# Where a chunked-attention and feed-forward kernel issues the adds of its second block's partial results

## The chip, the cores and the metric

The kernel runs on one core of a Trainium2 chip. The metric is the device time of one execution in microseconds (us); several executions are timed, and their median is given. Of one execution there is also a profile with a trace of every instruction and DMA.

## The reference

The attention works on chunks of 64 tokens (eight batches, eight heads, 576 tokens, head size 64); its output `x` has 4608 rows of 512, and goes through a feed-forward layer with a hidden size of 2048 and a PReLU:

```python
scores = scale * np.matmul(q_c, k_c.transpose(0, 1, 2, 4, 3))
scores = scores - np.max(scores, axis=-1, keepdims=True)
attn = np.exp(scores)
attn = attn / (np.sum(attn, axis=-1, keepdims=True) + 1e-09)
out = np.matmul(attn, v_c)
...
h = x @ w_in
g = np.maximum(h, 0.0) + alpha * np.minimum(h, 0.0)
return (g @ w_out).astype(np.float32)
```

## The kernel before

Tokens are worked on in nine blocks of 512. The first three ("plain" blocks 0, 1 and 2) compute the feed-forward layer directly; the other six are worked on in three pairs with a seven-product (Strassen-like) scheme, whose combined weights are made while the plain blocks run. All matrix products are done in three passes on values split into a high and a low part.

The plain part is a list of 48 steps `(phase, block, f)`: in one step `ffn_in` (L311) multiplies `x` with the f-th 128 columns of `w_in`, `prelu` (L300 to L303) and a split into `gh` and `gl` (L323, L324) follow on ScalarE and VectorE, and `ffn_out` (L336) of the step two places earlier adds into four PSUM banks `ps_o`. Blocks 0 and 1 take turns in four phases, since the weights arrive as they go: each is interrupted once, its four sums are put aside in DRAM (`partial`), and when the block's second part ends, the new sums are added to these by DMAs that GpSimd issues with `accum_op=add`. `store` (L345) copies the four banks into SBUF: the first two into the two halves of a buffer `more`, the third into `ob`, the fourth into `g`. The fourth is added at once (L374). The first three go into the list `adds` (L372) and are issued later, one at a time.

Beside these steps run, at fixed step numbers, "visits" (L396) of the attention of later blocks. A visit runs on TensorE the values product of the tile two visits back (L272, which reads the transposed probabilities `pT` and writes the two PSUM tiles `ps_a`) and the scores of a new tile (L194, into the same two tiles). Then come on VectorE the row maxima (L210) and their scaling (L211), on ScalarE eight exponentials (L214, each followed by a read of its sum), on VectorE the division (L216 to L218), on ScalarE a copy of the values' product out of PSUM (L288), on VectorE a transpose of 32 by 32 blocks (L225), and on SP's queue eight DMAs into `pT` (L232) and one load of `v`. The next visit writes both `ps_a` tiles anew, and so needs L214, L288 and L210 of the last to be done.

At the steps named in `COMBINE` (L806) `combine` (L512) makes two new weight tiles. It adds high and low parts of two tiles (L520), forms four combinations (L527 to L530), and for each of the two tiles casts it into a buffer (L536, ScalarE), puts the rest beside it (L537, VectorE) and stores its two halves to DRAM by two DMAs of GpSimd (L498 in `keep_a`). The buffer is one of two named `raw`, or `raw`, `raw`, `more` in rotation (L533) where `early` is false, so a cast waits until the stores of an earlier tile out of the same buffer have landed. Behind each tile's two stores one entry of `adds` is issued, if there is one:

```python
            for half, s in zip((left, right), name):
                stored = keep_a(side, {1: 5, 2: 6, 3: 7, 4: 3}[s], j, w[:, :, half])
            if adds:
                to, what = adds.pop(0)
                with tc.issue_after(stored.ins):
                    nc.gpsimd.dma_start(out=to, in_=what, accum_op=ALU.add)
```

The order on each engine is set by a list scheduler from priorities and its own model of durations; TensorE's part from step 20 on is pinned to the program's order. Each engine executes its list in order. GpSimd's DMAs run in one queue and share the chip's DMA engines with SP's and ScalarE's. The first block's three adds are issued in the combinations at steps 29 and 30, the second block's in those at steps 35 and 36; `wo_640`, `wo_705` and `wo_766` below belong to steps 36, 37 and 39.

Of the kernel before, what the change touches and what calls it, by code (L numbers as in the profile page):

```python
# [27 lines left out]
def tile_local_attention_prelu_ffn(  # L28
# [44 lines left out]
    def f32(t):  # L73
        return t.bitcast(F32)
# [66 lines left out]
    def prepare(f, behind=None):  # L141
        with tc.issue_after(behind.ins) if behind else nullcontext():
            wi[f] = split_weight("wi", f)
            wo[f] = split_weight("wo", f)
# [10 lines left out]
    def attn_load(s, parts="qkv", other=None):  # L155
        if "q" in parts:
            q_sb, kb = (load.tile([P, H, C], F32, name=name) for name in ("q_sb", "k_sb"))
            for t, src in ((q_sb, qT), (kb, kT)):
                (other or nc.sync).dma_start(out=t, in_=src[:, s].rearrange("p (h t) -> p h t", t=C))
            qkv[s] = [q_sb, kb, None]  # L160
        if "v" in parts:
            v_sb = load.tile([P, DM], F32, name="v_sb", bufs=2)
            loads.append(nc.sync.dma_start(out=v_sb, in_=v[:, s]))
            qkv[s][2] = v_sb
# [178 lines left out]
    adds = []  # L343

    def store(acc, b, keep):  # L345
        for t, o in enumerate(acc):
            rows = slice(b * TB + t * P, b * TB + (t + 1) * P)
            before = partial.get((b, t))
            if b == PLAIN - 1:
                ob = const.tile([P, DM], F32, name=f"wi{NF - 2 - t}")  # L350
            elif keep and b == 0:
                side = "wi" if t % 2 else "wo"
                ob = const.tile([P, DM], F32, name=f"{side}{NF - 1 - t // 2}")
            elif keep:
                pool, name = ((load, "q_sb"), (load, "v_sb"), (load, "v_sb"), (soft, "pr"))[t]
                ob = pool.tile([P, DM], F32, name=name, bufs=2 if name == "v_sb" else 1)
            elif t < 2:
                if t == 0:
                    both = stage.tile([P, 2, DM], F32, name="more", bufs=1)
                ob = both[:, t]  # L360
            elif t == 2:
                ob = stage.tile([P, DM], F32, name="ob", bufs=1)
            else:
                ob = gp.tile([P, DM], F32, name="g")
            with tc.high_priority(offset=HIGH):
                nc.scalar.copy(ob, o)  # L366
            if keep:
                partial[b, t] = dram.tile([P, DM], F32, name=f"partial{b}_{t}")
                nc.sync.dma_start(out=partial[b, t], in_=ob)
            elif before is not None:  # L370
                if t < 3:
                    adds.append((before, ob))  # L372
                else:
                    nc.gpsimd.dma_start(out=before, in_=ob, accum_op=ALU.add)  # L374
                finals.append((out[rows, :], before))
            else:
                nc.sync.dma_start(out=out[rows, :], in_=ob)

    def new_x():
        return (xp.tile([P, NK, TB], F32R, name="xh"), xp.tile([P, NK, TB], F32R, name="xl"))  # L380
# [6 lines left out]
    def attend(part, s):  # L387
        with tc.high_priority(offset=HIGH):
            if part == 0:
                attn_softmax(s, attn_scores(s))  # L390
            elif part == 1:
                attn_transpose(s) if s < EARLY else attn_blocks(s)
            else:
                attn_x(s, attn_values(s))
# [101 lines left out]
    def keep_a(side, i, j, a):  # L496
        n, u = unit(side, i, j)
        return nc.gpsimd.dma_start(out=units[side][n][:, u], in_=f32(a))  # L498
# [3 lines left out]
    def keep_quarters(f):  # L502

        j, second = f % JF, f >= JF
        keep_a("wi", 4 if second else 1, j, wi[f][:, :, halves[second]])
        keep_a("wo", 4 if second else 1, j, wo[f][:, :, halves[second]])
        if second:
            keep_a("wo", 2, j, wo[f][:, :, halves[0]])
        else:
            keep_a("wi", 2, j, wi[f][:, :, halves[1]])  # L510

    def combine(side, j, early):  # L512

        ws = wi if side == "wi" else wo
        pair = [ws[j], ws[JF + j]]
        left, right = halves
        a = []
        for w in pair:
            t = stage.tile([P, 512], F32, name="t1")
            nc.vector.tensor_tensor(t, f32(w[:, 0]), f32(w[:, 1]), op=ALU.add)  # L520
            a.append(t)
        a11, a22 = a[0][:, left], a[1][:, right]
        if side == "wi":
            a12, a21 = a[0][:, right], a[1][:, left]
        else:
            a21, a12 = a[0][:, right], a[1][:, left]
        nc.vector.tensor_tensor(a22, a21, a22, op=ALU.add)  # L527
        nc.vector.tensor_tensor(a21, a11, a21, op=ALU.subtract)
        nc.vector.tensor_tensor(a11, a22, a11, op=ALU.subtract)
        nc.vector.tensor_tensor(a12, a12, a11, op=ALU.subtract)  # L530
        names = ((2, 4), (3, 1)) if side == "wi" else ((2, 3), (4, 1))
        for t, name in zip(a, names):
            which = "raw" if early else ("raw", "raw", "more")[fetched[0] % 3]  # L533
            fetched[0] += 1
            w = stage.tile([P, 2, 512], F32R, name=which, bufs=2 if which == "raw" else 1)
            nc.scalar.copy(w[:, 0], t)  # L536
            nc.vector.tensor_tensor(w[:, 1], t, f32(w[:, 0]), op=ALU.subtract)  # L537
            for half, s in zip((left, right), name):
                stored = keep_a(side, {1: 5, 2: 6, 3: 7, 4: 3}[s], j, w[:, :, half])
            if adds:  # L540
                to, what = adds.pop(0)
                with tc.issue_after(stored.ins):
                    nc.gpsimd.dma_start(out=to, in_=what, accum_op=ALU.add)

# [247 lines left out]
    def new_raw(b):  # L792
        for n, name in enumerate(("xh", "xl")):
            x[b + n] = xp.tile([P, NK, TB], F32, name=name)

    COMBINE = (20, 22, 23, 24, 26, 29, 30, 31, 33, 35, 36, 37, 39, 40, 41, 43)
    combined = [(side, j) for side in ("wi", "wo") for j in range(JF)]
    ops, conversion = {}, []
    for n, (p, b, f) in enumerate(steps):
        _, f0, f1 = phases[p]  # L800
        if f == f0:
            acc = []
            if p >= 3 and b + 1 < PLAIN:
                x[b + 1] = new_x()
        if n == 2 * NF:
            new_raw(PLAIN)  # L806
        if n == n0 + 1:

            tick = nc.gpsimd.tensor_copy(out=table, in_=f32(x[1][1])[:, 0, TB - 1:])
        if n0 < n <= n0 + NF:  # L810
            with tc.issue_after(tick.ins):
                keep_quarters(n - n0 - 1)
        pinned[0] = n >= 20
        if n == len(steps) - 1:
            with tc.issue_after(loads[-1].ins):
                while finals:
                    dst, src = finals.pop(0)
                    nc.sync.dma_start(out=dst, in_=src)
        for st, s in beside[n]:
            attend(st, s)  # L820
        if 2 * n in late:
            if 2 * n == visits[0]:
                attn_load(late[2 * n][1], "q")
            visit(*late[2 * n])
        if ready < NF:
            prepare(ready, done_x.get({2: SPB, 3: SPB + 2, 4: SPB + 3}.get(ready)))
            ready += 1
        elif n in COMBINE:

            with tc.issue_after(stages["softmax"][0].ins), tc.issue_after(stages["softmax"][1].ins):  # L830
                combine(*combined.pop(0), 23 <= n <= 36)
        if n == len(steps) - 8:
            ops, conversion = convert(PLAIN)
        if len(steps) - 8 <= n < len(steps) - 4:
            conversion.pop(0)()
        pending.append((acc, ffn_in(x[b], f), f, f0, f1, b, False))
        if 2 * n + 1 in late:
            visit(*late[2 * n + 1])
        if n >= len(steps) - 3:

            with tc.issue_after(stages["split"][0].ins):
                for _ in range(3):
                    conversion.pop(0)()

        if len(pending) > (1 if n < 20 else 2):
            second(*pending.pop(0))
# [9 lines left out]
    for pair in range(NPAIR):  # L856
        b = PLAIN + 2 * pair
# [53 lines left out]
```

## Time and profile before

| | |
|---|---|
| median of three runs | 839.68 us |
| lowest and highest of them | 834.14 and 841.08 us |
| the profiled execution | 837.25 us |
| its span from first to last instruction | 835.5 us |
| TensorE matmul busy | 806.1 us (96%) |
| TensorE weight load busy | 644.8 us (77%) |
| VectorE busy | 671.0 us (80%) |
| ScalarE busy | 542.8 us (65%) |
| GpSimd busy | 215.7 us (26%) |
| moved by DMA | 192.40 MB, mean 230 GB/s |
| chain that ended last | TensorE 83%, ScalarE 4%, DMA 4%, VectorE 3%, SP's queue 3% |

The first line is what counts; the others are of one execution, whose times are read against its own 837.25 us. Matmuls overlap, so the shares say which engine is busy, not how near it is to its peak.

### The profile page before, as it was taken

The page shows a single profiled execution, that of the slowest core. Times are in us where ns is not written, and L with a number is a line of the kernel's source. Part 1 is how long each engine was busy: PE and PEld are TensorE (multiplying, and loading weights), DVE is VectorE, ACT ScalarE, POOL GpSimd, SP SyncE. Part 2 cuts the span into 40 slices and gives each one's busy share as a digit, 9 for nine tenths or more (in the row PEclk, how much of TensorE's full clock was granted, in tenths as well). Part 3 has the DMA queues.
Part 4 walks back from the last instruction along what each step waited for, and adds up shares of the span by engine and source line. Part 5 has one row for each costly group of instructions (what it writes and reads, how often), then busy time and mean ns, then how long its engine had stood idle before and what let it go on. Part 6 is the DMA issues. An engine that isn't in the chain of part 4 may idle for free.

```text
span 835.5 us, 15368 instructions
## 1 busy us (share of the span) xinstructions
PE 806.1 (96%) x5248; PEld 644.8 (77%) x5248; DVE 671.0 (80%) x1268; ACT 542.8 (65%) x1392; POOL 215.7 (26%) x340
## 2 busy tenths in 40 slices
PE   4799999999989899999999999999999999999998
PEld 3577888777768678787788788787887888888886
DVE  5899999979769888677688996777789966568875
ACT  5985666657666576677876555687765546566452
POOL 4006223224324432111112242111122422111232
PEclk9999999999999899999999999999999999999999
DMA  9629777656687868687876799786557995555788
GB/s 277 215 78 343 236 248 267 192 159 205 207 212 238 222 202 287 223 270 260 260 248 208 225 241 335 261 268 207 187 199 234 250 296 188 187 191 188 237 228 231
DMA packets 73966, 192.40 MB, mean 230 GB/s; under 512 B 11664, under 2 KB 19104, under 8 KB 73760
## 3 DMA queue, kind: packets, MB, share of 16 engines
q0 software_dynamic: 38272, 127.43, 48.7%
q1 hardware_dynamic: 27248, 48.91, 18.5%
q10 hardware_dynamic: 8368, 15.08, 5.6%
q8 instruction: 42, 0.69, 0.3%
q14 instruction: 36, 0.29, 0.1%
HBM read 135.27 MB, written 42.99 MB: 213 GB/s over the span
## 4 chain that ended last, share of the span: by engine, by line
PE 83%; ACT 4%; DMA 4%; DVE 3%; SPq 3%; issue 2%; ACTq 0%; POOL 0%; DVEq 0%
PE ps_o L623 19%; PE ps_o L756 15%; PE ps_h L756 12%; PE ps_h L311 12%; PE ps_o L336 12%; PE ps_h L623 9%; SPq L232 3%; DMA pT<-t 2%; PE ps_a L272 2%; PE ps_a L194 1%; DMA wi<-kT 1%; ACT wo L214 1%; ACT pr L214 1%; DMA wo_a<-raw 1%; ACT wi L214 1%
## 5 line engine op out<-in xcount | busy, mean ns | idle before, releaser
L336 PE MATMUL ps_o<-wo,gh 128*128 128x512 f32 x384 | 114.7, 397 | 1.2 <-ACT g L366 1.2
L311 PE MATMUL ps_h<-xh,wi 128*128 128x512 f32 x384 | 107.4, 402 | 1.8 <-DVE g L303 1.2
L311 PEld LDWEIGHTS ps_h<-xh,wi 128*128 128x128 f32 x384 | 72.0, 190 | 19.9 <-DVE g L303 1.7
L336 PEld LDWEIGHTS ps_o<-wo,gh 128*128 128x128 f32 x384 | 71.5, 188 | 19.1 <-ACT g L366 1.6
L214 ACT ACTIVATE pr<-ps_a,mx 128x64 f32<-128x64 f32 x224 | 67.3, 328 | 25.2 <-DVE mx L211 23.1
L336 PE MATMUL ps_o<-wo,gl 128*128 128x512 f32 x192 | 69.3, 396 | 0.1
L623 PE MATMUL ps_o<-wi,raw 128*128 128x512 f32 x171 | 67.9, 397 | 0.0
L623 PE MATMUL ps_o<-wo,raw 128*128 128x512 f32 x171 | 67.8, 396 | 0.0
L311 PE MATMUL ps_h<-xl,wi 128*128 128x512 f32 x192 | 53.4, 400 | 0.0
L561 POOL DMA_DIRECT2D raw<-wi_a x42 | 22.4, 532 | 106.4 <-PE ps_o L623 60.6
L214 ACT ACTIVATION_READ_ACCUMULATOR pr<-ps_a,mx 128x1 f32 x224 | 49.5, 221 | 0.0
L323 ACT CAST gh<-g 128x512 fp32r<-128x512 f32 x48 | 29.9, 622 | 28.9 <-DVE g L303 22.9
L301 ACT ACTIVATE wo<-gh 128x512 f32<-128x512 f32 x24 | 15.2, 634 | 50.4 <-DVE gh L646 50.4
L579 ACT CAST gh<-wi 128x512 fp32r<-128x512 f32 x45 | 28.1, 625 | 25.3 <-PE ps_o L756 10.3
L561 POOL DMA_DIRECT2D raw<-wo_a x42 | 22.4, 532 | 84.9 <-PE ps_o L756 44.0
L311 PEld LDWEIGHTS ps_h<-xl,wi 128*128 128x128 f32 x192 | 36.6, 191 | 8.7
L301 ACT ACTIVATE g<-ps_h 128x512 f32<-128x512 f32 x48 | 29.4, 613 | 21.1 <-PE ps_h L311 20.8
L336 PEld LDWEIGHTS ps_o<-wo,gl 128*128 128x128 f32 x192 | 35.9, 188 | 9.3 <-DVE gl L324 0.5
L623 PE MATMUL ps_o<-wi,wo 128*128 128x512 f32 x99 | 39.3, 397 | 0.0
L623 PE MATMUL ps_o<-wo,wo 128*128 128x512 f32 x99 | 39.1, 395 | 0.0
L623 PEld LDWEIGHTS ps_o<-wo,raw 128*128 128x128 f32 x171 | 32.2, 188 | 7.7
L623 PEld LDWEIGHTS ps_o<-wi,raw 128*128 128x128 f32 x171 | 32.1, 188 | 7.6
(251 smaller groups left out, 2285.3 us busy)
## 6 DMA issues: line engine op xcount, KB each, us to landing
raw<-wi_a POOLq DMA_DIRECT2D x42, 512.0 KB, 4.7
raw<-wo_a POOLq DMA_DIRECT2D x42, 512.0 KB, 4.7
wi<-wi_a POOLq DMA_DIRECT2D x21, 512.0 KB, 4.5
wo<-wi_a POOLq DMA_DIRECT2D x21, 512.0 KB, 4.7
wi<-wo_a POOLq DMA_DIRECT2D x21, 512.0 KB, 4.6
wo<-wo_a POOLq DMA_DIRECT2D x21, 512.0 KB, 5.1
v_sb<-v SPq DMA_DIRECT2D x28, 256.0 KB, 4.8
pT<-t SPq DMA_DIRECT2D x224, 32.0 KB, 4.0
```

The lines of the kernel that those rows point to most:

```text
L194: pe(nc.tensor.matmul(att[par][c * C:(c + 1) * C, (NP + hp) * C:(NP + hp + 1) * C], lhsT=q_sb[rows, 2 * hp + c], rhs=kb[rows, 2 * hp + c], ...
L214: last = nc.scalar.activation(pr[:, g], one, AF.Exp, bias=mx[:, g], scale=SCALE, accum_out=sm[:, g])
L232: nc.sync.dma_start(out=pT[dst, i].rearrange("p h t -> p (h t)"), in_=tb[src, j].rearrange("p h t -> p (h t)"),)
L272: pe(nc.tensor.matmul(att[c][par * C:(par + 1) * C, hp * C:(hp + 1) * C], lhsT=v_sb[rows, h * C:(h + 1) * C], rhs=p[rows, :, par * NP + hp ...
L301: nc.scalar.activation(g, h, AF.Relu, scale=-1.0)
L311: pe(nc.tensor.matmul(hps, lhsT=wi[f][:, l, k * P:(k + 1) * P], rhs=xx[:, k], start=(i == 0 and k == 0), stop=(i == 2 and k == NK - 1),))
L323: nc.scalar.copy(gh, g)
L336: pe(nc.tensor.matmul(o, lhsT=a[:, ts], rhs=wo[f][:, l], start=(f == first and i == 0), stop=(f == last and i == 2),))
L561: streamed[0] = nc.gpsimd.dma_start(out=f32(t), in_=units[side][n])
L579: hi = nc.scalar.copy(t_hi, t)
L623: pe(nc.tensor.matmul(ps, lhsT=w[:, l, k * P:(k + 1) * P], rhs=xx[:, xl], start=first and at == 0, stop=at == n - 1, skip_group_check=not ...
L756: pe(nc.tensor.matmul(ps[m], lhsT=w[:, l, m * P:(m + 1) * P], rhs=xx, start=i != 6 and j == 0 and n == 0, stop=j == JF - 1 and n == 2, ski ...
```

## The change

The entries of `adds` carry their block's number. An entry of the first block is issued as before, behind either tile's stores; an entry of the second block only behind the stores of a combination's second tile. The flag `early`, which keeps a combination to the two `raw` buffers, is given up to step 37 instead of 36.

```diff
@@ store
                 if t < 3:
-                    adds.append((before, ob))
+                    adds.append((b, before, ob))
@@ combine
-        for t, name in zip(a, names):
+        for at, (t, name) in enumerate(zip(a, names)):
...
-            if adds:
-                to, what = adds.pop(0)
+            if adds and (at == 1 or adds[0][0] == 0):
+                _, to, what = adds.pop(0)
                 with tc.issue_after(stored.ins):
                     nc.gpsimd.dma_start(out=to, in_=what, accum_op=ALU.add)
@@ the loop over the steps
-                combine(*combined.pop(0), 23 <= n <= 36)
+                combine(*combined.pop(0), 23 <= n <= 37)
```

The instruction lists of TensorE are the same. GpSimd's list from the first tile of step 35 on, before (`wo_a` are the stored halves in DRAM, `partial1_0` and so on the second block's sums there):

```order
L498 DMA wo_a16_395<-raw_3024 128x2x256
L498 DMA wo_a4_383<-raw_3024 128x2x256
L543 DMA partial1_0_1408<-more_2901 128x512
L498 DMA wo_a20_399<-raw_3030 128x2x256
L498 DMA wo_a12_391<-raw_3030 128x2x256
L543 DMA partial1_1_1412<-more_2901 128x512
L498 DMA wo_a17_396<-raw_3077 128x2x256
L498 DMA wo_a5_384<-raw_3077 128x2x256
L543 DMA partial1_2_1416<-ob_2904 128x512
L498 DMA wo_a21_400<-raw_3083 128x2x256
```

And from the same place in the changed kernel:

```order
L498 DMA wo_a16_395<-raw_3024 128x2x256
L498 DMA wo_a4_383<-raw_3024 128x2x256
L498 DMA wo_a20_399<-raw_3029 128x2x256
L498 DMA wo_a12_391<-raw_3029 128x2x256
L543 DMA partial1_0_1408<-more_2901 128x512
L498 DMA wo_a17_396<-raw_3076 128x2x256
L498 DMA wo_a5_384<-raw_3076 128x2x256
L498 DMA wo_a21_400<-raw_3081 128x2x256
L498 DMA wo_a13_392<-raw_3081 128x2x256
L543 DMA partial1_1_1412<-more_2901 128x512
```

Each combination's four stores now follow one another, with one add behind them; the third add stands behind the stores of step 37.

ScalarE's list around the two casts of step 36, before (`t_3069` and `t_3071` are the tiles that are cast, `wi_3644` an operand of the later blocks):

```order
L302 ACTIVATE g<-g,alpha_sb 128x512
L536 CAST raw<-t_3069 128x512
L301 ACTIVATE g<-ps_h 128x512
L579 CAST wi_3644<-xh 128x512
L536 CAST raw<-t_3071 128x512
L323 CAST gh<-g 128x512
L302 ACTIVATE g<-g,alpha_sb 128x512
```

And in the changed kernel (`t_3068` and `t_3070` are the same two tiles):

```order
L302 ACTIVATE g<-g,alpha_sb 128x512
L536 CAST raw<-t_3068 128x512
L536 CAST raw<-t_3070 128x512
L301 ACTIVATE g<-ps_h 128x512
L579 CAST wi_3644<-xh 128x512
L323 CAST gh<-g 128x512
L302 ACTIVATE g<-g,alpha_sb 128x512
```

The second cast moved up past L301 and L579, directly behind the first.

VectorE's list from the first L537 of step 36 to the L211 of the visit, before:

```order
L537 TENSOR_TENSOR raw<-t_3069,raw 128x512
L580 TENSOR_TENSOR wi_3644<-xh,wi_3644 128x512
L520 TENSOR_TENSOR t_3191<-wo_705 128x512
L537 TENSOR_TENSOR raw<-t_3071,raw 128x512
L324 TENSOR_TENSOR gl<-g,gh 128x512
L210 TENSOR_REDUCE mx<-ps_a 128x4 x2
L303 SCALAR_TENSOR_TENSOR g<-ps_h,g 128x512
L520 TENSOR_TENSOR t_3193<-wo_1235 128x512
L211 TENSOR_SCALAR mx<-mx 128x8
```

And in the changed kernel:

```order
L537 TENSOR_TENSOR raw<-t_3068,raw 128x512
L537 TENSOR_TENSOR raw<-t_3070,raw 128x512
L580 TENSOR_TENSOR wi_3644<-xh,wi_3644 128x512
L520 TENSOR_TENSOR t_3190<-wo_705 128x512
L324 TENSOR_TENSOR gl<-g,gh 128x512
L520 TENSOR_TENSOR t_3192<-wo_1235 128x512
L303 SCALAR_TENSOR_TENSOR g<-ps_h,g 128x512
L210 TENSOR_REDUCE mx<-ps_a 128x4 x2
L527 TENSOR_TENSOR t_3192<-t_3190,t_3192 128x256
L211 TENSOR_SCALAR mx<-mx 128x8
```

The second L537 moved up past L580 and L520, and the second L520 and L303 now stand ahead of L210. Elsewhere on VectorE and ScalarE some neighbouring instructions change places, up to the end of the third block.

## Rows read from the trace of the kernel before

**Rows 1.** The page's 40 slices of the span: TensorE's busy tenths.

```profile
PE   4799999999989899999999999999999999999998
```

**Rows 2.** TensorE in order of time from 282: start us, us, engine, line, count, [idle].

```profile
282.12 0.40 PE L336 MATMUL ps_o<-wo,gl 128*128 128x512 f32 x1
284.64 0.33 PE L272 MATMUL ps_a<-pT,v_sb 64*64 64x64 f32 x2 [2.12 <-ACT xl L288]
286.19 1.02 PE L272 MATMUL ps_a<-pT,v_sb 64*64 64x64 f32 x27 [1.23 <-DVE raw L537]
...
288.10 2.07 PE L311 MATMUL ps_h<-xh,wi 128*128 128x512 f32 x4
...
293.00 0.63 PE L336 MATMUL ps_o<-wo,gh 128*128 128x512 f32 x2
```

**Rows 3.** Stretches: us, busy PE, PEld, DVE, ACT, POOL; granted clock, DMA share, GB/s.

```profile
20.00:22.50 2.50, 0.35 (x5) 0.14 (x4) 1.55 (x7) 2.50 (x12) 0.00 (x0) 1.00 1.06 293
22.90:26.20 3.30, 3.30 (x28) 2.64 (x26) 2.35 (x7) 3.26 (x16) 0.00 (x0) 0.50 1.07 313
33.00:36.00 3.00, 1.15 (x20) 0.91 (x20) 2.75 (x7) 2.96 (x16) 0.00 (x0) 1.00 0.35 91
36.00:40.00 4.00, 3.33 (x29) 2.69 (x26) 1.77 (x5) 4.00 (x23) 0.00 (x0) 1.00 0.60 200
...
288.00:292.00 4.00, 4.00 (x15) 3.13 (x10) 3.75 (x8) 1.43 (x3) 1.45 (x2) 0.50 0.81 225
```

**Rows 4.** TensorE in order of time at an earlier visit.

```profile
214.72 0.63 PE L272 MATMUL ps_a<-pT,v_sb 64*64 64x64 f32 x27 [0.43 <-DVE xl L298]
...
215.80 1.20 PE L311 MATMUL ps_h<-xh,wi 128*128 128x512 f32 x4
...
218.71 0.63 PE L336 MATMUL ps_o<-wo,gh 128*128 128x512 f32 x2
```

**Rows 5.** ScalarE in order of time from 273 to 285.

```profile
273.91 0.67 ACT L301 ACTIVATE g<-ps_h 128x512 f32<-128x512 f32 x1
...
277.92 0.62 ACT L536 CAST raw<-t 128x512 fp32r<-128x512 f32 x1 [2.84 <-DMA wo_a<-raw]
...
284.18 0.68 ACT L288 COPY xl<-ps_a 128x256 f32<-128x256 f32 x2
```

**Rows 6.** VectorE in order of time from 275 to 282.

```profile
275.14 0.68 DVE L537 TENSOR_TENSOR raw<-t,raw 128x512 fp32r<-128x512 f32 x1
275.74 0.69 DVE L580 TENSOR_TENSOR wi<-xh,wi 128x512 fp32r<-128x512 f32 x1
...
279.79 0.75 DVE L210 TENSOR_REDUCE mx<-ps_a 128x4 f32<-128x256 f32 x2
...
281.65 0.17 DVE L211 TENSOR_SCALAR mx<-mx 128x8 f32<-128x8 f32 x1
```

**Rows 7.** GpSimd in order of time: the issues of the second block's three adds.

```profile
270.05 0.95 POOL L543 DMA_DIRECT2D partial<-more x1
...
272.08 1.35 POOL L543 DMA_DIRECT2D partial<-more x1
...
277.55 0.98 POOL L543 DMA_DIRECT2D partial<-ob x1
```

**Rows 8.** DMA pairs by line: ns of the issue, first and last start, landing.

```profile
L498 POOL DMA_DIRECT2D wo_a<-raw x2: 725/726/727, 268.6 to 269.3; - x2
DMA to landing us min/median/max: 3.0/3.0/3.0
...
L498 POOL DMA_DIRECT2D wo_a<-raw x2: 1087/1096/1105, 270.6 to 271.4; - x2
DMA to landing us min/median/max: 6.5/6.5/6.6
...
L232 SPq DMA_DIRECT2D pT<-t x2: 507/548/589, 279.2 to 279.8; - x2
DMA to landing us min/median/max: 6.1/6.1/6.2
```

## Prediction

> **What bounds the kernel now.** I read the page's slices first, then the stretches by engine, then TensorE in order of time, then ScalarE, VectorE, GpSimd and the DMA landings of the same few microseconds. TensorE is busy in nearly the whole span [rows 1]; between its start and its last slice only two are not at 9, the 12th and the 14th (of about 21 us each), and both lie where the change works. The reader should see one hole in the 14th. TensorE begins its last L336 matmul at 282.12 (done by 282.52), waits 2.12 us, runs two small ones at 284.64, waits another 1.23 us, and resumes only at 286.19 [rows 2]. Its granted clock then stands at 0.50 between 288 and 292 [rows 3], that is at 1.2 instead of 2.4 GHz.
>
> What that clock costs is read from rows at both levels. From the resumed L272 to the first L311 took 288.10 - 286.19 = 1.91 us, and the twelve L311 matmuls took 293.00 - 288.10 = 4.90 us [rows 2]. The same steps at full clock took 215.80 - 214.72 = 1.08 and 218.71 - 215.80 = 2.91 us [rows 4]. So the lower clock costs 0.83 + 1.99 = 2.8 us. Waiting and clock together are 2.12 + 1.23 + 2.8 = 6.2 us. That is the most this place can give back, 0.7% of the time.
>
> Why did TensorE wait? The small matmuls L272 overwrite the PSUM tiles that ScalarE must first empty (softmax L214, then copy L288 at 284.18 [rows 5]); L214 needs VectorE's L211, which ran at 281.65 [rows 6]. Both engines were late because ScalarE stood 2.84 us before the cast L536 at 277.92, waiting until the stores out of the same buffer had landed [rows 5]. VectorE's second L537 waits for that cast. The stores had been issued at 270.6 and 271.4, behind an add issued at 270.05 [rows 7], and took 6.5 us to land; the pair ahead of the add took 3.0 us [rows 8]. The second wait, until 286.19, is named after VectorE, but the matmul also reads pT: its last two DMAs were issued at 279.2 and 279.8 and took 6.1 and 6.2 us [rows 8], so the last one landed at 279.8 + 6.2 = 286.0. I take pT to be what ended last there.
>
> **The change, part by part.** *The add between the halves' stores goes away* for the second block's three results. At the first of these combinations (step 35) the second pair of stores follows the first at once: issues at 269.3 + 0.73 = 270.05 and 270.8. Landing takes 3.0 us if nothing is in front, as for the first pair, and 6.5 us if the delay was not the add's [rows 8]; so the buffer is free between 273.8 and 277.3, against 271.4 + 6.5 = 277.9 before. I take 273.8, the nearer row: same buffer, same size, same queue, 1.5 us earlier.
>
> *ScalarE and VectorE are reordered by the scheduler*, as the second and third piece of the instruction lists show. The cast now stands directly behind its predecessor, ahead of L301, which began at 273.91 [rows 5]. With the buffer free at 273.8 the cast begins about then and costs L301 one place, 0.5 us, with nobody waiting on it. On VectorE the two L537 stand together: 275.14 and then 275.74, the pitch of this kind of instruction being 0.60 us [rows 6]. L580, L520, L324, L520 and L303 come next at that pitch, so L210 starts at 275.74 + 6 x 0.60 = 279.34. In the old order L211 came 281.65 - 279.79 = 1.86 us behind L210, with L303 and L520 (1.2 us) in between; now one L527 stands between, at most another 0.60. So L211 runs at 279.34 + 0.66 + 0.60 = 280.6 instead of 281.65, 1.05 us earlier. The new order itself gives part of the gain away, since L520 and L303 now stand ahead of L210. ScalarE's softmax and copy follow at their old distance (284.18 - 281.65 = 2.53), so L288 begins at 283.1, and the first L272 can start at 284.64 - 1.05 = 283.6, the second half at about 283.9 with the second copy.
>
> *pT* then decides. Its transpose and DMAs are issued before anything that is moved, so its last issue stays near 279.8. Before, an add issued at 277.55 [rows 7] was still in flight then; in the changed kernel the second add comes behind the four stores of step 36, at about 279.0, and one add fewer has been started by then. From below, pT lands as quickly as the undisturbed stores, 3.0 us, at 282.8; from above it lands 6.2 us later as before, at 286.0, and beyond, if the add hurts it more (the last rival). I take 283.8, nearer the lower end, because one whole add has left the preceding stretch.
>
> So TensorE resumes its second half at about 284.0 instead of 286.19: 2.2 us. The wait shrinks from 3.35 us to somewhat under 2. Whether the clock then falls is read from two earlier places. Between 20.0 and 22.5 TensorE was busy for 0.35 of 2.5 us, and the clock from 22.9 to 26.2 was 0.50; between 33 and 36 it was busy for 1.15 of 3 us, a hole of 1.85, and the clock stayed 1.00 [rows 3]. A wait of under 2 us that is split in two by some matmuls is nearer the second, so I take the 2.8 us as saved. **Sum: 2.2 + 2.8 = 5.0 us.** From 288 on every slice reads 9 [rows 1]: TensorE has no later hole for the gain to fall into, and its own instructions are the same in number and order.
>
> *Edits that cost nothing.* The three adds are not removed but issued later, the second from 272.08 [rows 7] to about 279, the third by some 10 us to behind step 37. Nobody reads the sums until the last step of the third block, and the buffer `more` that holds two of them is next written at step 39; if that cover went, the cast at step 39 would wait as the one at step 36 did, 2.84 us. GpSimd issues the same number of DMAs. The flag for step 37 moves nothing: in both lists step 37 writes the two `raw` buffers, since the rotation gave those already. SP's list differs in the place of one output DMA near the end of the third block, far from TensorE's path.
>
> One rule of the Trainium skill speaks against part of this. DMA: Bandwidth & Descriptors, section "Queues, rings and completion order", says that each DMA engine goes round between the queues a packet at a time, while inside one queue descriptors start in order. The first half says that pT, which is on SP's queue, never had to sit behind GpSimd's adds as a whole; by it pT's landing would not move and the sum would be near nothing (the second rival). The trace agrees with the second half (6.5 us behind the add, 3.0 ahead of it), and leaves the first open, since pT did take 6.2 us.
>
> **Rivals.** (1) *The clock falls all the same.* The place at 20 us shows that 2.15 us without work was enough [rows 3]. Then only 2.2 us are gained: 835.1. The skill's TensorE: Matmul & The Clock Gate, section "What's actually happening", says that the moment at which activity is judged isn't tied to the kernel's start; by that the same gap may be followed by a fall in one execution and not in the next.
> (2) *pT holds TensorE as before.* For it: it landed last at 286.0. Against it: an add less in flight. TensorE resumes at 286.2 and the hole and the clock stay: 0 gained, 837.3.
> (3) *The moved add makes pT later, and the kernel slower.* Four stores in a row and the add are issued from 276 to 280, just where pT's last two DMAs and the loads of the next q and k are. If these then take about 8 us instead of 6.2, TensorE resumes at 288 and the time is 2 us longer: 839.3. It decides as soon as pT lands after 286.0.
>
> **How the numbers follow.** The profiled execution took 837.25 us (its span is 835.5); the median of the three runs, 839.68, lies 2.4 us above it, and the four times together average 838.1. Against the profiled time the forecast is 837.25 - 5.0 = 832.3, against the mean of the four 833.1; I give 833. The forecast has a chance of 0.55, rivals (1), (2) and (3) have 0.20, 0.15 and 0.10. The likeliest case alone spans 831 to 835. All rivals lie between 835 and 839.3 on the profiled time, 1 us more on the mean; with the scatter of the three runs (834.14 to 841.08) the range is 828.5 to 840.5. One per cent is 8.4 us, about what a measurement of this kernel can tell from no change. No case reaches it: the place gives at most 6.2 us, and the slower rival costs 2. Faster by over 1% therefore needs the forecast and luck with the runs, 0.10; slower by over 1% needs rival (3) and bad luck, 0.04; the rest, 0.86, is within 1%.
>
> **What would show it.** Right: the second pair of stores of step 35 landing within about 3.5 us; no wait before the second L536 of step 36; L211 about a microsecond earlier; TensorE back between 283.5 and 284.5; the clock at 1.00 from 284 to 296. Wrong: the stores still taking over 6 us without the add ahead of them (then the delay was not the add's); TensorE idle until pT lands at 286; a clock of 0.50 after a hole of less than 2 us; or a new hole at one of the next two visits, at 301 or 311, because VectorE lost the time in which it caught up.

## The result and the profile after

The changed kernel takes 840.74 us (median of 22 runs, 838.82 to 843.37) against 838.73 us of the kernel before in the same session (22 runs, 834.14 to 842.32). The ratio is 1.003, with a 95% interval of 1.0018 to 1.0041: some 2 us slower, where 5 us less was forecast. The profiled execution took 841.0 us, its span is 839.2 us.

The page's slices do not show a difference of this size: the 12th and the 14th slice of TensorE read 8, as in [rows 1], and all behind them 9. TensorE in order of time does (start us, us, engine, line, tiles, count, idle time before and its releaser), and answers to [rows 2]:

```profile
282.77 0.40 PE L336 MATMUL ps_o<-wo,gl 128*128 128x512 f32 x1
284.54 0.33 PE L272 MATMUL ps_a<-pT,v_sb 64*64 64x64 f32 x2 [1.38 <-ACT xl L288]
286.45 0.63 PE L272 MATMUL ps_a<-pT,v_sb 64*64 64x64 f32 x27 [1.58 <-ACT raw L536]
...
287.53 1.82 PE L311 MATMUL ps_h<-xh,wi 128*128 128x512 f32 x4
...
291.98 0.62 PE L336 MATMUL ps_o<-wo,gh 128*128 128x512 f32 x2
...
309.08 1.10 PE L311 MATMUL ps_h<-xh,wi 128*128 128x512 f32 x4
311.69 0.95 PE L272 MATMUL ps_a<-pT,v_sb 64*64 64x64 f32 x29 [1.51 <-ACT xl L288]
```

The two waits before the visit at 286 are still there, 1.38 + 1.58 = 2.96 us instead of 3.35, and a third of 1.51 us has come at the visit of 310, where the kernel before had none. The stretches (busy time, then granted clock, DMA share and GB/s) answer to [rows 3]:

```profile
284.20:287.80 3.60, 1.68 (x65) 1.50 (x66) 3.20 (x7) 2.71 (x7) 1.46 (x2) 1.00 0.56 151
288.00:291.00 3.00, 3.00 (x9) 2.32 (x8) 3.00 (x9) 0.62 (x1) 2.41 (x3) 0.50 0.86 251
292.00:296.00 4.00, 4.00 (x19) 3.25 (x18) 1.36 (x4) 4.00 (x17) 0.00 (x0) 1.00 1.03 286
```

The clock still falls to 0.50, but later: the stretch up to 287.80 reads 1.00, and the 27 L272 take 0.63 us as at full clock [rows 4], where the kernel before took 1.02 [rows 2]. The twelve L311 matmuls took 291.98 - 287.53 = 4.45 us, against 4.90 in [rows 2] and 2.91 at full clock in [rows 4]. From the end of the last L336 to the next one the hole takes 291.98 - 283.17 = 8.81 us, against 293.00 - 282.52 = 10.48 before: 1.67 us gained (0.39 of waiting, 1.28 of clock). At 310, measured in the same way from the end of the last L311 to the first L336 behind the visit, the changed kernel takes 313.09 - 310.18 = 2.91 us and the one before 312.22 - 311.20 = 1.02: 1.89 us lost, 1.51 of it the printed wait. So the two places together give nothing in this pair of executions (0.22 us lost).

They do not make up the difference of the two spans, though (839.2 against 835.5 us). Matched matmul by matmul, TensorE of the changed kernel is 0.6 us behind the kernel before at 282, 1.0 ahead at 293, 0.9 behind at 312, and still 0.9 behind at 400, but 3.4 behind from 450 on. The 2.6 us between arise from 416 to 442, in several small stops that the kernel before does not have. The largest:

```profile
421.76 0.50 PE L623 MATMUL ps_o<-wi,raw 128*128 128x512 f32 x1 [0.85 <-ACT g L644]
```

The trace of `behind_43_again` below has this stop too (0.84 us), that of `again`, the same kernel as here, has none. So they go with the execution, and no run shows that the change causes them.

GpSimd's issues, which answer to [rows 7]:

```profile
269.66 2.90 POOL L498 DMA_DIRECT2D wo_a<-raw  x4 [3.85 <-DVE mx L211]
272.56 0.96 POOL L543 DMA_DIRECT2D partial<-more  x1
...
280.21 0.97 POOL L543 DMA_DIRECT2D partial<-more  x1
```

And the landings, answering to [rows 8] (the last three of step 35's four stores, then the last two pT DMAs):

```profile
L498 POOL DMA_DIRECT2D wo_a<-raw x3: 727/727/727, 270.4 to 271.8; - x3
DMA to landing us min/median/max: 3.1/3.1/3.2
...
L232 SPq DMA_DIRECT2D pT<-t x2: 1152/1378/1604, 279.6 to 280.8; - x2
DMA to landing us min/median/max: 5.3/5.3/5.3
```

The stores behind the first now land in 3.1 us instead of 6.5, as forecast (3.0). The last pT lands at 280.8 + 5.3 = 286.1, and TensorE resumes at 286.45: the releaser that is printed, ScalarE's L536, writes nothing that L272 reads. The second add is issued at 280.21, beside the last pT DMA.

VectorE, first at the visit of 286 (answering to [rows 6]), then on the way to the one of 310:

```profile
276.35 1.28 DVE L537 TENSOR_TENSOR raw<-t,raw 128x512 fp32r<-128x512 f32 x2
...
281.55 0.16 DVE L211 TENSOR_SCALAR mx<-mx 128x8 f32<-128x8 f32 x1
...
297.50 0.71 DVE L225 STREAM_TRANSPOSE t<-pr 128x512 f32<-128x512 f32 x1 [2.77 <-DMA v_sb<-v]
...
304.68 0.69 DVE L537 TENSOR_TENSOR raw<-t,raw 128x512 fp32r<-128x512 f32 x1 [0.23 <-ACT raw L536]
305.29 0.75 DVE L210 TENSOR_REDUCE mx<-ps_a 128x4 f32<-128x256 f32 x2
...
307.16 0.17 DVE L211 TENSOR_SCALAR mx<-mx 128x8 f32<-128x8 f32 x1
```

ScalarE, the casts of step 36 (answering to [rows 5]) and the softmax for the visit of 310:

```profile
274.61 1.20 ACT L536 CAST raw<-t 128x512 fp32r<-128x512 f32 x2
...
307.27 0.62 ACT L579 CAST wo<-xh 128x512 fp32r<-128x512 f32 x1 [2.10 <-DVE t L520]
...
310.61 0.77 ACT L302 ACTIVATE g<-g,alpha_sb 128x512 f32<-128x512 f32 x1
311.22 0.69 ACT L288 COPY xl<-ps_a 128x256 f32<-128x256 f32 x2
```

The kernel before at the same visit, VectorE, ScalarE and TensorE:

```profile
297.16 0.71 DVE L225 STREAM_TRANSPOSE t<-pr 128x512 f32<-128x512 f32 x1
...
303.45 0.75 DVE L210 TENSOR_REDUCE mx<-ps_a 128x4 f32<-128x256 f32 x2
...
304.71 0.17 DVE L211 TENSOR_SCALAR mx<-mx 128x8 f32<-128x8 f32 x1
```

```profile
307.24 0.68 ACT L288 COPY xl<-ps_a 128x256 f32<-128x256 f32 x2
```

```profile
311.13 0.69 PE L272 MATMUL ps_a<-pT,v_sb 64*64 64x64 f32 x32
```

Before, L288 began 3.9 us ahead of TensorE's L272 (in the second trace of that kernel too). After, it begins at 311.22, when TensorE has been waiting for a microsecond (from 310.18). Three things in the new lists stand behind it. L225 comes ahead of both L537 of step 39 instead of between them, so that both stand behind its wait of 2.77 us for DMAs of the visit before. L537 comes ahead of L210. On ScalarE, L579 comes ahead of the softmax and stands there for 2.10 us until VectorE's L520 is done, and L302 comes ahead of L288: from L211 to L288 it takes 311.22 - 307.16 = 4.06 us instead of 307.24 - 304.71 = 2.53. This distance hardly depends on the execution: it is 2.53 and 2.54 us in the two traces of the kernel before, 4.05 or 4.06 in the five of kernels with the changed order, and 3.00 or 3.01 in the seven with the order mended (the table below tells which these are).

### The profile page after: what moved, and what is told of

It reads as the page before. It is cut to its first block, busy times and chain, and to the rows that moved or that the text cites. A ratio compares the mean times of both kernels' runs of the same rounds, so it can differ in the third digit from the quotient of the medians.

```text
span 839.2 us, 15368 instructions
## 1 busy us (share of the span) xinstructions
PE 806.1 (96%) x5248; PEld 643.2 (77%) x5248; DVE 671.4 (80%) x1268; ACT 543.3 (65%) x1392; POOL 216.0 (26%) x340
## 4 chain that ended last, share of the span: by engine, by line
PE 67%; ACT 9%; DVE 9%; DMA 7%; SPq 3%; issue 3%; POOL 1%; DVEq 0%; ACTq 0%; POOLq 0%
PE ps_o L756 14%; PE ps_o L623 13%; PE ps_h L756 12%; PE ps_h L311 10%; PE ps_o L336 9%; PE ps_h L623 6%; SPq L232 3%; DMA pT<-t 3%; ACT pr L214 3%; DMA v_sb<-v 2%; PE ps_a L272 1%; DMA k_sb<-kT 1%; DMA raw<-w_out 1%; DVE t L225 1%; ACT wo L214 1%
## 5 line engine op out<-in xcount | busy, mean ns | idle before, releaser
L336 PE MATMUL ps_o<-wo,gh 128*128 128x512 f32 x384 | 114.5, 396 | 0.5 <-ACT g L366 0.5
L311 PE MATMUL ps_h<-xh,wi 128*128 128x512 f32 x384 | 108.1, 404 | 1.7 <-DVE g L303 1.4
L311 PEld LDWEIGHTS ps_h<-xh,wi 128*128 128x128 f32 x384 | 72.4, 191 | 20.3 <-DVE g L303 2.5
L336 PEld LDWEIGHTS ps_o<-wo,gh 128*128 128x128 f32 x384 | 71.6, 188 | 18.0 <-ACT g L366 0.9
L336 PE MATMUL ps_o<-wo,gl 128*128 128x512 f32 x192 | 69.2, 396 | 0.0
L311 PE MATMUL ps_h<-xl,wi 128*128 128x512 f32 x192 | 53.4, 400 | 0.0
L301 ACT ACTIVATE wo<-gh 128x512 f32<-128x512 f32 x24 | 15.2, 634 | 50.7 <-DVE gh L646 50.7
L579 ACT CAST gh<-wi 128x512 fp32r<-128x512 f32 x45 | 28.1, 624 | 25.2 <-PE ps_o L756 10.9
L311 PEld LDWEIGHTS ps_h<-xl,wi 128*128 128x128 f32 x192 | 36.6, 191 | 8.7
L336 PEld LDWEIGHTS ps_o<-wo,gl 128*128 128x128 f32 x192 | 35.9, 188 | 8.8 <-issue 0.3
L301 ACT ACTIVATE g<-ps_h 128x512 f32<-128x512 f32 x48 | 29.4, 613 | 19.2 <-PE ps_h L311 18.9
```

The costliest lines, as they stand in the source:

```text
L301: nc.scalar.activation(g, h, AF.Relu, scale=-1.0)
L311: pe(nc.tensor.matmul(hps, lhsT=wi[f][:, l, k * P:(k + 1) * P], rhs=xx[:, k], start=(i == 0 and k == 0), stop=(i == 2 and k == NK - 1),))
L336: pe(nc.tensor.matmul(o, lhsT=a[:, ts], rhs=wo[f][:, l], start=(f == first and i == 0), stop=(f == last and i == 2),))
L579: hi = nc.scalar.copy(t_hi, t)
```

## The experiments

Each kernel was timed in five rounds against the kernel before on the same chip; waits are those of its profiled execution. The theories that the first expectations name: by the *order theory* the scheduler's new order at steps 39 and 40 makes L288 late at 310, and eats what is won at 286; by the *traffic theory* the moved adds hold up pT at 286; by the *chance theory* the waits fall here or there from one execution to the next whatever the lists say. The later expectations also name a *two-cause theory*, which takes the first two together.

The traces are of single executions and not always of a typical one: those of `adds_behind_37` (842.82 us) and `behind_43_again` (840.40) are of the slowest of their twelve.

| kernel | order at step 40 | second block's adds | waits at 286, us | wait at 310, us | median, us | ratio to before, 95% |
|---|---|---|---|---|---|---|
| `before_again` | old | 35, 36 | 1.42 + 2.81 | none | 838.75 | 0.9987 to 1.0023 |
| `again` | changed | 35, 36, 37 | 1.30 + 2.54 | 0.95 | 839.21 | 0.9982 to 1.0029 |
| `l225_behind` | mended | 35, 36, 37 | 1.02 + 1.67 | none | 839.42 | 0.9987 to 1.0031 |
| `no_second_adds` | changed | left out | 1.24 | 2.39 | 838.89 | 0.9980 to 1.0030 |
| `adds_at_once` | changed | near 250 | none, 1.79 at 253 | 2.40 | 841.56 | 1.0002 to 1.0052 |
| `behind_43_old_order` | changed | 43 | 1.86 | 2.45 | 839.59 | 0.9986 to 1.0027 |
| `placed_no_adds` | mended | left out | 1.48 | none | 835.48 | 0.9953 to 0.9995 |
| `adds_behind_37` | mended | 37 | 1.77 | none, 1.22 at 300 | 840.31 | 1.0010 to 1.0044 |
| `adds_behind_39` | mended | 39 | 1.77 | 0.79 | 839.40 | 0.9994 to 1.0033 |
| `adds_behind_43` | mended | 43 | 0.63 | 0.25 | 834.96 | 0.9934 to 0.9972 |
| `adds_one_each_late` | mended | 40, 41, 43 | 1.57 | none | 835.00 | 0.9944 to 0.9976 |
| `behind_43_again` | mended | 43 | 1.94 | 0.43 | 837.05 | 0.9954 to 0.9994 |

**The two kernels a second time** (`again`, `before_again`, no edit).

> The changed kernel once more, for a second trace. Order theory (ScalarE's and VectorE's new order around steps 39 to 43 makes the copy L288 late for the visit near 311): a wait of about 1.5 us before L272 near 311 again, and the time 2 to 3 us over the kernel before. Traffic theory (the moved adds delay pT): pT lands last again before the visit near 286, with a wait of about 3 us there. Chance theory (the first trace had waits that others don't have): the wait near 311 is gone, and the time is within 1 us of the kernel before.

> The kernel before, unchanged, as a control and as a second trace. All theories: ratio 1.000 with an interval that holds 1. Order and two-cause theories: the waits of 2.1 and 1.2 us before the visit at 286 and the lower clock behind them are there again, and none over 0.5 us at 310. Chance theory (where the wait falls is a matter of the execution, not of the lists): the waits stand at another visit, or are twice as long or half as long.

The kernel before gave a ratio of 1.0005 to itself. Its second trace has the hole at the same place, and this time the profile names pT (TensorE in order of time):

```profile
283.65 0.33 PE L272 MATMUL ps_a<-pT,v_sb 64*64 64x64 f32 x2 [1.42 <-ACT xl L288]
286.79 1.02 PE L272 MATMUL ps_a<-pT,v_sb 64*64 64x64 f32 x27 [2.81 <-DMA pT<-t]
```

The changed kernel again waits at 310 (0.95 us), the one before again does not. So the places of the waits go with the lists; their lengths vary by a microsecond and more between executions, and in that the chance theory is right. The second ratio of the changed kernel, 1.0005, has an interval that overlaps the first one between 1.0018 and 1.0029: the loss is nothing to some 0.3%.

**The order at step 40 mended** (`l225_behind`): the transpose L225 of the visit that step 40 calls (TensorE runs it near 286) is held behind the second L537 of the combination at step 39. On the lists this brings L225 behind the two L537 of step 39, L210 ahead of those of step 40, and L579 and L302 behind L288; behind that visit, up to the next one, more instructions of VectorE and ScalarE change places.

```diff
-            nc.vector.tensor_tensor(w[:, 1], t, f32(w[:, 0]), op=ALU.subtract)
+            stages["low"] = nc.vector.tensor_tensor(w[:, 1], t, f32(w[:, 0]), op=ALU.subtract)
...
-            if new is not None:
-                attn_blocks(new)
+            with tc.issue_after(stages["low"].ins) if new == EARLY + 11 else nullcontext():
+                if new is not None: attn_blocks(new)
```

> The changed kernel, with the transpose L225 of the visit near 286 held behind the last L537 of step 39, which also brings L210 ahead of L537 at step 40 and L579 behind the softmax, as in the kernel before. The DMAs are those of the changed kernel. Order theory: the wait near 311 goes, 1.5 us less than the changed kernel, and the time is then within 1.5 us of the kernel before. Traffic theory: no change against the changed kernel, 2 to 3 us over the kernel before.

The wait at 310 is gone: L288 begins at 308.21, with L579 behind it (ScalarE in order of time).

```profile
308.21 0.69 ACT L288 COPY xl<-ps_a 128x256 f32<-128x256 f32 x2
308.73 0.70 ACT L579 CAST wo<-xh 128x512 fp32r<-128x512 f32 x1
```

Yet the time is 839.42, no better than `again` (839.21), where the order theory had 1.5 us less: TensorE still waits at 286 in two parts. The second is printed as a wait for ScalarE's L536, but the last pT lands at 286.4 (issued at 281.60, 4.8 us).

```profile
284.79 0.33 PE L272 MATMUL ps_a<-pT,v_sb 64*64 64x64 f32 x2 [1.02 <-ACT xl L288]
286.78 0.63 PE L272 MATMUL ps_a<-pT,v_sb 64*64 64x64 f32 x27 [1.67 <-ACT raw L536]
```

**The adds taken away, and put elsewhere, in the changed order** (`no_second_adds`, `adds_at_once`). VectorE's and ScalarE's lists of instructions are those of the changed kernel.

```diff
-                    adds.append((b, before, ob))
+                    adds.append((b, before, ob)) if b == 0 else None
```

```diff
-                if t < 3:
+                if t < 3 and b == 0:
```

> The changed kernel without the second block's three adds: the sums of three quarters of its second part are left out. Each engine's list is otherwise that of the changed kernel. Traffic theory: pT lands 1.5 us or more earlier before the visit near 286, the wait there falls under 2 us, the clock stays up, and the time is 3 to 5 us under the changed kernel. Order theory: the wait near 311 stays at about 1.5 us, and the time is within 2 us of the changed kernel.

> The changed kernel with the second block's three adds issued at once when the sums have been copied out, near 250, instead of behind steps 35 to 37. Each engine's list is otherwise that of the changed kernel. Traffic theory: as without the adds near 286 (wait under 2 us), with perhaps a new wait near 262 or 273 where the three adds now run: 0 to 4 us under the changed kernel. Order theory: the wait near 311 stays, and the time is within 2 us of the changed kernel.

Without the adds the visit at 286 is one piece, its L272 all start together (TensorE, `no_second_adds`), and the last two pT DMAs land in 3.4 and 4.3 us:

```profile
284.37 0.95 PE L272 MATMUL ps_a<-pT,v_sb 64*64 64x64 f32 x29 [1.24 <-ACT xl L288]
...
309.54 1.00 PE L272 MATMUL ps_a<-pT,v_sb 64*64 64x64 f32 x29 [2.39 <-ACT xl L288]
```

```profile
L232 SPq DMA_DIRECT2D pT<-t x2: 987/1032/1076, 279.5 to 280.6; - x2
...
DMA to landing us min/median/max: 3.4/3.9/4.3
```

The queue that by its bytes carries the stores and the adds took this share of the 16 engines' time from 268 to 292 (packets, MB, share), first in the changed kernel, then without the adds:

```profile
q0 software_dynamic: 1172, 3.42, 52.4%
```

```profile
q0 software_dynamic: 896, 2.95, 36.2%
```

So the adds (three are issued in these 24 us, the last at 289.91) take 16.2 points of it, 3.9 us of all sixteen engines. In the four traces with adds beside it the last pT DMA took 4.8 to 6.1 us (`before`, `before_again`, the changed kernel, `l225_behind`), in the seven without them whose trace holds its landing 3.4 to 4.5. But what is won at 286 stands at 310 as a wait of 2.39 us, and the time is 838.89, not the 3 to 5 us under the changed kernel that the traffic theory had. With the adds at once the same split visit, named after pT, appears where they now run, and the wait at 310 is there too (TensorE, `adds_at_once`):

```profile
253.43 0.63 PE L272 MATMUL ps_a<-pT,v_sb 64*64 64x64 f32 x27 [1.79 <-DMA pT<-t]
...
311.75 0.95 PE L272 MATMUL ps_a<-pT,v_sb 64*64 64x64 f32 x29 [2.40 <-ACT xl L288]
```

This kernel took 841.56 us, 2.35 over `again` on the same chip, where the order theory had at most 2 either way and the traffic theory none: with the adds put earlier there is a second costly visit.

So each cause alone may be removed without any gain. The next runs remove both.

**Both removed** (`placed_no_adds`: the edits of `l225_behind` and `no_second_adds`).

> The changed kernel with two edits: at step 40 the visit's VectorE and ScalarE work stands behind the combination's first low part (as in l225_behind), and the second block's three adds are left out altogether (the sums of the first three banks of that block lack their first part), so that GpSimd's queue holds only stores there. Two-cause theory (the adds keep pT late at 286, the new order makes L288 late at 310, each about 2.5 to 5 us): no wait over 0.5 us at the second half of the visit at 286, none at 310, no fall of the clock at either, and 834 to 836 us, 3 to 5 us under the changed kernel. Traffic-alone theory (whatever else moves on the DMA engines holds pT, not the adds): the wait at 286 is there, 838 to 839. Compensation theory (VectorE is behind by a fixed amount, and TensorE waits for it somewhere, whatever the order): a wait of 1 to 2.5 us appears at another visit between 286 and 345, 837 to 839.

One wait of 1.48 us is left at 283, none at 300 or 310, and the time is 835.48 us, ratio 0.9974: the only combination of the four that gains. A theory by which the loss only wanders to another visit falls with it.

**The adds back in, in the mended order** (`adds_behind_37`, `adds_behind_39`, `adds_behind_43`, `adds_one_each_late`). The edits also keep the tiles of more steps (up to 39, 40, 43 and 43) in the two buffers `raw`, since `more` holds two of the sums longer. The edit for the third:

```diff
-            if adds and (at == 1 or adds[0][0] == 0):
+            for _ in range(0 if not adds else 1 if adds[0][0] == 0 else 3 * (at == 1 and side == "wo" and j == 7)):
...
-                combine(*combined.pop(0), 23 <= n <= 37)
+                combine(*combined.pop(0), 23 <= n <= 43)
```

> Computes the whole reference. As l225_behind, and the second block's three adds stand one behind another behind the stores of step 37 (around 291 us), the flag early given up to step 39; nothing else of the lists moves. Two-cause theory: pT of the visit at 286 lands by 284.5 since no add is in flight, no second wait there; the three adds run from 291 to 296, and if they make the next pT (due at 300) late, a wait of about 1 us comes there; 834.5 to 837 us. Traffic-alone theory: the wait at 286 stays at 1.5 to 2.5 us, 838 to 840. Compensation theory: no wait at 286, one of 1 to 2.5 us at 300 or 310, 837 to 839.

> Computes the whole reference. As adds_behind_37, with the three adds behind the stores of step 39 and the flag early given up to step 40, so that the tiles of steps 37 to 40 use the two buffers alone. Two-cause theory: no second wait at 286, as with the adds left out; the adds then run near 300 to 306, where the visit at 310 reads its pT: a wait of up to 2 us at 310 if they delay it, else none; 834.5 to 837.5 us. Traffic-alone theory: the wait at 286 stays, 838 to 840. Compensation theory: a wait of 1 to 2.5 us at 310 named after ScalarE's L288, 837 to 839.

> Computes the whole reference. As l225_behind, with the second block's three adds one behind another behind the stores of step 43 (near 328 us, where VectorE has slack and no visit follows closely), and the flag early given up to step 43, so that all tiles of steps 37 to 43 use the two buffers alone; the third block's output DMAs that read these sums move behind the next pT. Two-cause theory (the adds' traffic holds whichever tight visit they run beside; the order makes L288 late at 310): no second wait at 286, none at 300 or 310, so as with the adds left out, 834.5 to 837 us. If the two buffers alone make the casts of steps 39 to 41 wait for stores, a wait of 0.8 us at 310 stays, as in adds_behind_39: 837 to 838.5. Compensation theory (the adds cost about 4 us wherever they stand): a wait or a fall of the clock at 330 to 345 or at the visit behind it, 838.5 to 841.

> Computes the whole reference. As adds_behind_43, with the three adds one behind each of the combinations at steps 40, 41 and 43 (near 310, 317 and 328 us). Two-cause theory: the first add runs beside pT of the visit after 310, which is not due before 323, so no wait at 286, 300 or 310: 834.5 to 837 us. Compensation theory: 838.5 to 841, with a wait at 310 or at the visit behind it.

In all four the second wait at 286 is gone. Behind step 37 the three adds hold pT of the next visit, behind step 39 that of the one after (TensorE of the one and of the other):

```profile
300.90 0.63 PE L272 MATMUL ps_a<-pT,v_sb 64*64 64x64 f32 x27 [1.22 <-DMA pT<-t]
303.02 2.08 PE L311 MATMUL ps_h<-xh,wi 128*128 128x512 f32 x4 [0.97 <-DVE g L303]
```

```profile
310.58 0.69 PE L272 MATMUL ps_a<-pT,v_sb 64*64 64x64 f32 x30 [0.79 <-DMA pT<-t]
```

These two came out at 840.31 and 839.40, above the 834.5 to 837 and 834.5 to 837.5 that the two-cause theory gave them; a wait there was expected, its price was not. Behind step 43 the adds meet a pT as well (GpSimd, SP's queue and TensorE of `adds_behind_43`), but one that is issued from 321.34 and, by the program (a visit reads the pT of the tile two visits back), first read at 352.40:

```profile
324.33 1.85 POOL L543 DMA_DIRECT2D partial<-more  x2
325.50 1.57 POOL L543 DMA_DIRECT2D partial<-ob  x1
```

```profile
321.34 7.94 SPq L232 DMA_DIRECT2D pT<-t  x8
```

```profile
285.69 1.02 PE L272 MATMUL ps_a<-pT,v_sb 64*64 64x64 f32 x29 [0.63 <-ACT xl L288]
...
308.53 0.94 PE L272 MATMUL ps_a<-pT,v_sb 64*64 64x64 f32 x29 [0.25 <-ACT xl L288]
...
352.40 0.69 PE L272 MATMUL ps_a<-pT,v_sb 64*64 64x64 f32 x32
```

It takes 834.96 us, ratio 0.9953, and is faster than the kernel before by half a per cent; one add behind each of steps 40, 41 and 43 does the same (835.00, 0.9960).

A part of these gains is the clock's. Over all their executions the mean granted clock is 0.9951 to 0.9965 in the four rows of the table that gain, against 0.9933 to 0.9938 in the kernel before beside them. A difference of 0.0018 to 0.0027 is 1.5 to 2.3 us of full clock in 838 (an estimate), of gains of 2.2 to 3.2 us.

**Is the order needed for it?** (`behind_43_old_order`, the adds' edit without the one at step 40; `behind_43_again`, both edits a second time.)

> Computes the whole reference. As adds_behind_43 but without the edit at step 40: VectorE and ScalarE have the changed kernel's order there. Two-cause theory: no second wait at 286, but a wait of 1 to 2.5 us at 307 to 310 named after ScalarE's L288, with or without a fall of the clock behind it, as with the adds left out in that order: 837.5 to 839.5 us, 2.5 to 4 us over adds_behind_43. Adds-alone theory (the place of the adds is all that counts, the order at step 40 nothing): 834.5 to 836 us and no wait over 0.5 us at 310.

> adds_behind_43 a second time, beside the one in the old order. Two-cause theory: 834.5 to 836 us, ratio to before 0.994 to 0.998, no wait over 0.5 us at 300 or 310. If the gain of the first time was the chip's, the ratio is 0.998 to 1.002.

On one chip 839.59 us without and 837.05 us with the order mended: 2.5 us, about the wait of 2.45 us that stands at 310 in the first. (The means of the twelve times each differ by 2.3 us, with a 95% interval of 0.5 to 4.2.) The second median is one microsecond above the 834.5 to 836 expected, but on a chip where the kernel before took 839.28; the interval of its ratio, 0.9954 to 0.9994, does not reach 1, and overlaps that of the first time from 0.9954 to 0.9972. The kernel in the old order, which has the adds and the buffers of `adds_behind_43`, gains nothing (1.0006), so neither of these suffices alone.

## Why the prediction was wrong

**The stores, right.** Without the add between them the second pair landed in 3.1 us (3.0 forecast, 6.5 before).

**The new order on VectorE and ScalarE, right as far as it was followed.** The second L536 follows the first without a wait. The step's first store is issued at 269.66 instead of 268.6, so the whole place runs 1.06 us later here; L211 at 281.55 instead of 281.65 and the first L272 at 284.54 instead of 284.64 are then 1.16 us earlier against it (1.05 forecast).

**pT, wrong: the term of 2.2 us.** It rested on "one whole add has left the preceding stretch". Two adds were still in it, and the second moved from 272.08 to 280.21, behind the four stores, next to pT's last issue at 280.8. I had placed it at 279.0 and pT's last issue at 279.8, and so had the neighbourhood in the numbers, and took the lower end all the same. Landing took 5.3 us, not 4. With the adds out of the way it takes 3.4 to 4.3 us, so the mechanism was right and the change does not use it. The prediction's second rival (pT holds TensorE as before) is what happened here: 286.45 against 286.19. The sign of the third, pT landing after 286.0, was met by 0.1 us, but in a place that runs some 1 us later, and the two waits were not longer than before. The Trainium skill, DMA: Bandwidth & Descriptors, section "Queues, rings and completion order", has each engine go round between queues by packets; from this the prediction worked out that pT would not move, as a rule against its own sum. The runs do not bear that out: pT does feel the adds beside it, 5.3 us with them in flight, 3.4 to 4.3 without.

**The clock, wrong in part: the term of 2.8 us.** The clock fell, after two waits of under 2 us (the first rival). It cost 4.45 - 2.91 = 1.54 us instead of 2.8, so 1.28 was gained. That part is luck: the sum had the clock stay up, and behind the hole of 1.85 us near 35, from which it took this, the clock fell in the second trace of the same kernel (last section).

**"TensorE has no later hole for the gain to fall into", wrong, and the costliest.** A slice of 21 us that reads 9 can hold up to 2 us of waiting (the changed kernel's 15th has the wait of 1.51 and reads 9), and it does not say how near TensorE was to waiting. The visit of 310 was safe because L288 ran 3.9 us ahead of TensorE, and TensorE came late because of the hole at 286. The new lists take that lead away from both sides: L211 comes later, and L288 comes 4.06 us behind it instead of 2.53. I had read "elsewhere some neighbouring instructions change places" as harmless. "A new hole at 311" stood among the signs of a wrong forecast, but for another reason (VectorE losing the time in which it caught up), and with no price.

**The sum.** Of 5.0 us forecast, 1.67 came at 286 and 1.89 went at 310. `no_second_adds` shows the larger form of it: without the second wait at 286, TensorE waits 2.39 us at 310, and the median gains nothing. Two smaller readings were off without a weight in the sum: the 12th slice (230 to 251 us) lies ahead of the adds that are moved, and the four times average 838.0, not 838.1.

**Still open.** The two places explain why nothing was gained, not the 2 us of the first comparison; in that pair of traces most of the difference lies at 416 to 442, where its cause is open. The second comparison (1.0005) leaves the loss between nothing and 0.3%. The repeats of the two kernels have 1.30 + 2.54 + 0.95 = 4.79 us of waits after and 1.42 + 2.81 = 4.23 before, the clock not counted, which is the right sign, from one execution each. Which of the three moves at step 40 (L225, L210 or ScalarE's L579 and L302) makes L288 late was not tried apart.

## What to carry to other kernels

A wait that is taken from the bounding engine is a gain only up to the slack of the next place at which that engine waits for others: read there, for the kernel before, how far the producer ran ahead (here 3.9 us), and then walk the new lists from the change to that place. When a scheduler orders the code, an edit of one queue's place moves neighbours on other engines, and those moves belong to the sum. A transfer that nobody waits for still has a price for the transfers beside it, so put it where those have slack (here 40 us later), not one step further on.

## What the runs showed of the hardware

The fall of the clock does not follow the length of the wait. Behind waits of about the same length it fell in one execution and stood in the other, here at the visit of 310 (the stretch from 300 to 315 of `no_second_adds`, wait 2.39 us, and of `behind_43_old_order`, wait 2.45 us; the last but two numbers are the granted clock):

```profile
300.00:315.00 15.00, 12.61 (x106) 9.99 (x105) 14.01 (x30) 8.90 (x29) 5.78 (x8) 0.89 0.68 216
```

```profile
300.00:315.00 15.00, 12.55 (x113) 9.94 (x112) 13.97 (x31) 9.38 (x29) 5.79 (x8) 1.00 0.66 211
```

In one and the same kernel it did both, too: behind a hole of 1.85 us (1.86 in the second trace) before the L260 matmuls at 35 us the clock stood in the trace of `before` and fell in that of `before_again`:

```profile
35.50:38.50 3.00, 2.06 (x20) 1.69 (x21) 1.92 (x5) 2.98 (x15) 0.00 (x0) 1.00 0.78 255
```

```profile
35.50:38.50 3.00, 3.00 (x19) 2.48 (x18) 1.90 (x5) 3.00 (x17) 0.00 (x0) 0.50 0.76 247
```

So the saving of a shorter wait has a second part, a chance of the clock's price, and neither "under 2 us" nor the split in two decides it. The Trainium skill, TensorE: Matmul & The Clock Gate, section "What's actually happening", says that the moment of judgement is not tied to the kernel's start; the rows agree with that.
